# Reordered third-group products and DMA-turned q and k of unit 2 in a gated linear attention with a GEGLU block

## The chip, the cores and the metric

One core of a Trainium2 chip runs the whole program. The metric is the device time of one execution in microseconds (us). The engines are TensorE (PE; its weight loads are shown as PEld), VectorE (DVE), ScalarE (ACT), GpSimd (POOL) and SyncE (SP). SP and POOL also issue the DMAs; each issues in its own order.

## The reference

A recurrence over 768 steps for each of 4 batches and 8 heads of width 48, then a gated feed-forward block over the 3072 tokens that come out of it:

```python
mag = sqrt(a_re**2 + a_im**2)
a = (a_re + 1j * a_im) * min(mag, 0.999) / (mag + 1e-6)
for t in range(S):
    S_state = a[t][:, None] * S_state + outer(k[t], v[t])
    y[t] = q[t] @ real(S_state)
x = y as (B * S, 384)
g = x @ w_gate
gelu = 0.5 * g * (1 + erf(g / sqrt(2)))
ffn = (gelu * (x @ w_val)) @ w_out
out = x + sigmoid(x @ w_res) * ffn
```

The feed-forward width is 1536. All inputs are float32; the result is within the reference's type and shape, 3072 x 384 float32.

## The kernel before

**Groups and units.** The 768 steps of a batch are cut into three sections of 256 steps, two chunks of 128 each. A section of a batch is a *group*; there are 12, ordered by section and then by batch, so groups 0 to 3 are the first sections. Groups are gathered in *units*: unit 0 is group 0, unit 1 is groups 1 and 2, unit 2 is 3 and 4, unit 3 is 5 and 6, and so on, and unit 6 is group 11.

**The gates.** In a chunk the recurrence becomes a masked attention with q and k scaled by products of gates. The gates are handled as logarithm and angle. `squares` (lines L212 to L230) makes the sum of squares of a_re (tile `ar`) and a_im (tile `ai`): two squares, of which ScalarE does both for groups 0 and 5 and later, and one VectorE add into `lm`. `p1_steps` takes logarithms, a ratio and `p1_arctan` its arctangent. `cs_l` and `cs_t` sum logarithms and angles along the chunk by TensorE (L266, L299, L301); ScalarE turns the first sum into the tiles `E` and `Ei` and, by `p2_sin`, the second into sine and cosine, `CS`. The square of a_im of groups 5 and later is held in a buffer with the tag "E", of which there are two; `E` of each group and the square of earlier groups in the ramp use the same tag or others in turn.

**Products.** `products(g)` multiplies q by `E` (L360), k by `Ei` (L365), and each of these by `CS` into a padded tile of 128 columns per head, `padQ` and `padK` (L372). Two pads of each kind exist, used by even and odd groups.

**Attention.** It needs q and k with the step along the free axis. For groups below `TURN`, TensorE transposes them, four heads at a time (L450 for Q, L453 for K), into PSUM; ScalarE copies the Q half (L455) and VectorE the K half (L456) into SBUF, and then four score products follow (L460) and a mask (L463). From group `TURN` on, `products` issues on SP one transposing DMA for each pad (L376, tiles `QT` and `KT`), and the score products read those (L437, mask L440). Attention of groups below `TURN` is traced at high priority, that of later groups is not. The first unit has an attention of its own, `attention_first`, whose last masked score is remembered as `T["last"]`.

**Feed-forward.** For each unit and each of the 12 slices of the feed-forward width, `gv_step` makes a gate product `gp` (L586), a value product `vp` (L590), the gelu on ScalarE (L139, `h<-gp`) and a product on VectorE (L593), remembered as `T["gelu"]` and `T["gmul"]`. `rp_step` makes the residual gate (L602), and `op_step` the output product (L610), its scaling (L613), a store on SP (L617) and an accumulating store of x on POOL (L619).

**Stages and order.** After a ramp, the program runs for each unit u a phase X and a phase Y. Phase X of u holds the output products of unit u - 1, the second half of unit u's attention, the exponentials, angles and sines of unit u + 1, and the logarithms and arctangents of unit u + 2. Phase Y of u holds unit u's `gv_step`s, the products of unit u + 1 (`dec3` and `products`), the squares of unit u + 3 and the first half of unit u + 1's attention. `weave` merges the streams of a phase by hand: each stream has a begin and an end between 0 and 1, and its steps are spread between them. This written order gives priorities; the framework then puts the instructions of each engine into a fixed order at build time, in which an instruction may pass one of higher priority that isn't ready by the framework's own reckoning. On the chip each engine keeps that order. ScalarE's functions need table loads (L624), and `act` chains them so that they keep the written order.

**Fences in the order.** `issue_after(i)` puts the instructions that a block traces on i's engine behind i in that engine's queue; `paced(nm)` does so with the instruction remembered under a name, if there is one, and otherwise does nothing. It adds no wait between engines.

**Loads.** `load_a` (L159), `load_q` (L167) run on SP, `load_v` (L173) on POOL, the latter behind a one-element copy that waits for k's landing (L196, `landed`). The gate tiles have 4 (`ar`) and 6 (`ai`) buffers, q and k three each.

Of the kernel before, what the change touches and what calls it, by code (L numbers as in the profile page):

```python
# [16 lines left out]
def weave(*streams):  # L17

    order = []
    for si, (begin, end, steps) in enumerate(streams):  # L20
        n = len(steps)
        for i, step in enumerate(steps):
            order.append((begin + (end - begin) * (i + 0.5) / n, si, i, step))
    for _, _, _, step in sorted(order, key=lambda e: e[:3]):
        step()
# [3 lines left out]
def kernel(  # L29
# [23 lines left out]
    NG = B * NS  # L53
    UNITS = [[0]] + [[g, g + 1] for g in range(1, NG - 1, 2)] + [[NG - 1]]
    NU = len(UNITS)
# [2 lines left out]
    CHUNK = [b * NS + s for b, s in ORD]  # L58
    NEXT = {g: ORD.index((b, s + 1)) for g, (b, s) in enumerate(ORD) if s < NS - 1}
    P1AT = {2: -1}  # L60
    DVSQ = (1, 2, 3, 4)
    MAGIC = 12582912.0
    I2PI = 1.0 / (2.0 * math.pi)
    TURN = 5
    LATE0, LATE1 = 0.6, 1.0
    LNMAX = 0.5 * math.log(0.998001)

# [87 lines left out]
    def load_a(g, after=None):  # L155
        for nm, src, pool in (("ar", a_re, ldr), ("ai", a_im, lda)):
            t = pool.tile([128, C, H, D], FP, tag=nm, name=nm)
            for c in range(C):
                T["ld", nm, g] = held(nc.sync.dma_start(out=t[:, c], in_=rows(src, g, c)), after)  # L159
            T[nm, g] = t  # L160
        T["a"] = g + 1
# [71 lines left out]
    def p1_steps(g):  # L233

        def s0():
            lm = T["lm", g]
            act(out=lm, in_=lm, func=AF.Ln)
            nc.vector.tensor_scalar(out=lm, in0=lm, scalar1=0.5, scalar2=LNMAX, op0=OP.mult, op1=OP.min)  # L238

        def s1():  # L240
            ar = flat(T["ar", g])
            T["s", g] = pE.tile([128, W], FP, tag="E" if g == 1 else "Ei", name="ra") if g in (1, 2) else ar
            act(out=T["s", g], in_=ar, func=AF.Ln)

        def s2():
            T["th", g] = flat(T["ai", g])
            act(out=T["s", g], in_=T["s", g], func=AF.Exp, scale=-1.0)
            nc.vector.tensor_tensor(out=T["th", g], in0=T["s", g], in1=T["th", g], op=OP.mult)
        return [s0, s1, s2]

    def p1_arctan(g):
        act(out=T["th", g], in_=T["th", g], func=AF.Arctan)
# [374 lines left out]
    def gs(u):  # L627
        return UNITS[u] if 0 <= u < NU else []
# [7 lines left out]
    def call(f, *a):  # L636
        return lambda: f(*a)
# [4 lines left out]
    def att_steps(u, half):  # L642

        todo = [(g, c, i * C + c) for i, g in enumerate(gs(u)) for c in range(C)]
        n = len(todo) // 2
        steps = []
        for i, (g, c, jj) in enumerate(todo[half * n:half * n + n]):
            steps += attention(g, c)
            if i > 0:
                steps.insert(-1, call(xt_step, u, jj - 1))  # L650
        if n:
            steps.append(call(xt_step, u, half * n + n - 1))
        return steps

    def phase_x(u):

        pend = []
        g1 = gs(u + 1)
        p1g = [g for w in range(NU) if P1AT.get(w, w - 2) == u for g in gs(w)]
        now = [g for g in p1g if g in g1]  # L660
        ahead = [g for g in p1g if g not in g1]
        ops = [call(op_step, u - 1, jj) for jj in range(len(gs(u - 1)) * C)]
        att = att_steps(u, 1)
        if not g1:
            weave((0.0, 0.8, att), (0.1, 1.0, ops))
            return

        def csl(g, c):
            pend.append(cs_l(g, c))

        def ex():
            pend.pop(0)()

        def p1(g):
            return p1_steps(g) + [call(decay0, g)]
        csls = [call(csl, g, c) for g in g1 for c in range(C)]
        exs = [ex for _ in g1 for _ in range(C)]
        dec = [call(decay2, g) for g in g1]
        cst = [f for g in g1 for f in [call(carry, g)] + [call(cs_t, g, c) for c in range(C)]]
        sin = [call(p2_sin, g) for g in g1]  # L680
        table("natural_log_exp_and_others")()
        if now:
            atn = [table("trig_and_small")] + [call(p1_arctan, g) for g in now + ahead]
            pn = zip_steps([p1(g) for g in now])
            weave((0.0, 0.05, pn[:2]), (0.06, 0.1, csls), (0.12, 0.25, pn[2:]), (0.26, 0.4, exs),
                  (0.28, 0.48, zip_steps([p1(g) for g in ahead])),
                  (0.5, 0.5, dec), (0.55, 0.65, atn), (0.62, 0.8, cst), (0.9, 0.95, sin),
                  (0.0, 0.8, att), (0.0, 0.25, ops) if u == 1 else (0.1, 1.0, ops))
            return
        atn = [table("trig_and_small")] + [call(p1_arctan, g) for g in ahead]  # L690
        weave((0.0, 0.12, csls), (0.05, 0.5, zip_steps([p1(g) for g in ahead])), (0.12, 0.45, exs),
              (0.46, 0.46, dec), (0.2, 0.65, cst), (0.7, 0.95, atn + sin), (0.0, 0.8, att), (0.1, 1.0, ops))

    def ramp():

        g0, g1, g2 = gs(0) + gs(1)
        pend = {}

        def csl(g):
            pend[g] = [cs_l(g, c) for c in range(C)]  # L700

        def ex(g):
            for f in pend[g]:
                f()
            decay2(g)

        def cst(g):
            for c in range(C):
                cs_t(g, c)
        g3, g4 = gs(2)  # L710
        p = {g: p1_steps(g) for g in range(5)}
        q = {g: squares(g) for g in range(5)}
        pr = products(g0)

        def run(*fs):
            for f in fs:
                f()
        table("natural_log_exp_and_others")()
        run(*q[g0], p[g0][0], p[g0][1])
        csl(g0)  # L720
        run(p[g1][1], p[g0][2], q[g1][1], p[g1][2])
        ex(g0)
        run(p[g2][1], q[g2][1], p[g2][2])
        table("trig_and_small")()
        pr[0]()
        pr[2]()
        for g in (g0, g1, g2):
            if g > g0:
                T["f", g] = flat(T["ar", g])
            p1_arctan(g)  # L730
            cst(g)
            if g == g0:
                run(q[g1][0], q[g1][2], q[g2][0], q[g2][2])
        p2_sin(g0)
        pr[1]()
        pr[3]()
        a0 = attention_first(g0, 0, 0)
        table("natural_log_exp_and_others")()
        run(p[g1][0], p[g2][0])
        run(*a0[:2])  # L740
        csl(g1)
        csl(g2)
        run(*a0[2:4], *q[g3], p[g3][1], p[g3][2])
        ex(g1)
        run(*a0[4:7], *q[g4], p[g4][1])
        ex(g2)
        run(p[g4][2], p[g3][0], p[g4][0], call(decay0, g4), *a0[7:])
        with tc.issue_after(T["row"].ins):
            load_q(2, T["ld", "w", 2])
        load_w_out()  # L750
        table("trig_and_small")()
        p2_sin(g1)
        p2_sin(g2)
        with tc.issue_after(T["ld", "k", 2].ins):
            load_a(5)
        p1_arctan(g3)
        p1_arctan(g4)

    def phase_y(u):

        gv = []
        if 0 <= u < NU:
            table("gelu_and_others")()
            gv = [call(gv_step, u, f) for f in range(KF)]
            rp = [call(rp_step, u, jj) for jj in range(len(gs(u)) * C)]
            gv = gv[:8] + rp[:len(rp) // 2] + gv[8:] + rp[len(rp) // 2:]
        def late(f):
            with tc.issue_after(T["last"].ins):
                f()
        dec3 = [call(decay3, g) for g in gs(u + 1)]  # L770
        sq = [f for w in range(NU) if P1AT.get(w, w - 2) == u + 1 for g in gs(w) for f in squares(g)]
        pr = [st for g in gs(u + 1) for st in products(g)]
        if u == 0:
            pr = [call(late, f) for f in pr]
        weave((0.0, 1.0, gv), (0.0, 0.4, pr), (0.55, 0.56, dec3), (0.5, 0.95, sq), (0.3, 0.95, att_steps(u + 1, 0)) if u < 2 else (LATE0, LATE1, att_steps(u + 1, 0)))

    for g in range(3):
        load_a(g)
# [11 lines left out]
    for u in range(NU + 1):  # L790
        if u > 0:
            phase_x(u)
        while T["a"] < min(NG, gs(u + 1)[-1] + 6 if gs(u + 1) else NG):
            load_a(T["a"])
        phase_y(u)
        for g in gs(u + 2):
            with tc.issue_after(T["turn"].ins) if "turn" in T else nullcontext():
                load_q(g)
            after_landing(T["k", g], call(load_v, g))


# [28 lines left out]
```

## Time and profile before

Eight runs gave a median of 302.65 us (301.96 to 303.57). The profiled execution took 302.10 us by the same measure, of which 300.3 us are the span of the trace.

| engine | busy us | share of the span | instructions |
|---|---|---|---|
| PE | 256.7 | 85% | 1928 |
| DVE | 229.3 | 76% | 412 |
| ACT | 200.2 | 67% | 333 |
| POOL | 89.3 | 30% | 133 |

The mean granted clock of TensorE is 0.949 of full speed. The DMA queues moved 41.92 MB, 140 GB/s in the mean, nearly all in pieces under 512 B. The gelu tables are loaded at 57.11, 94.16, 138.36, 177.67, 218.68 and 252.96 us for units 0 to 5: these mark the stages. In the page's slices each digit is the busy share of a slice of 7.5 us in tenths; in a timeline the bracket behind a line gives the engine's idle time before it and what ended that. A busy PE is a PE with matmuls in flight, not one at its peak.

### The profile page before, as it was taken

What the parts mean: (1) busy time and instruction counts of PE and PEld (TensorE: products, weight loads), DVE (VectorE), ACT (ScalarE), POOL (GpSimd) and SP (SyncE); (2) the same over time, 40 slices, a digit from 0 to 9 for tenths busy, and PEclk for the clock granted to TensorE, in tenths of its full rate; (3) what the DMA queues carried; (4) which work ended last, traced back from release to release, by engine and by line L of the source; (5) the groups of instructions that cost most, each with busy time, mean ns of one, the idle gap of its engine ahead of it and who ended that gap; (6) DMA issues with size and microseconds to landing.
All of it is one profiled execution on the core that took longest, in us unless ns stands there. A gap on an engine that the chain in (4) does not pass through costs nothing.

```text
span 300.3 us, 5306 instructions
## 1 busy us (share of the span) xinstructions
PE 256.7 (85%) x1928; PEld 155.3 (52%) x1928; DVE 229.3 (76%) x412; ACT 200.2 (67%) x333; POOL 89.3 (30%) x133
## 2 busy tenths in 40 slices
PE   0345865599698999799999999989999998999994
PEld 0122543587354666454466654556545664455782
DVE  0789983989589999599897998888977776564452
ACT  3877788459989578996669964678464655445250
POOL 4020940400245520372113672125711222010220
PEclk9999575589979999999999999999999999999999
DMA  9999999999999993059999689998599735910631
GB/s 149 187 175 187 174 203 180 169 176 173 180 167 183 192 192 18 4 112 202 185 176 163 53 122 199 201 173 66 82 198 197 111 40 119 180 26 2 157 57 53
DMA packets 167427, 41.92 MB, mean 140 GB/s; under 512 B 156516, under 2 KB 167400, under 8 KB 167400
## 3 DMA queue, kind: packets, MB, share of 16 engines
q1 hardware_dynamic: 132424, 30.95, 62.1%
q0 software_dynamic: 34976, 10.63, 34.3%
q8 instruction: 15, 0.25, 0.3%
q14 instruction: 12, 0.10, 0.1%
HBM read 31.33 MB, written 9.08 MB: 135 GB/s over the span
## 4 chain that ended last, share of the span: by engine, by line
PE 67%; ACT 14%; DMA 8%; issue 4%; DVE 3%; SPq 2%; POOL 1%; ACTq 0%; DVEq 0%
PE op L610 15%; PE gp L586 15%; PE vp L590 14%; DMA q<-in_q_dram 4%; PE cst L299 4%; PE rp L602 3%; PE cst L301 3%; DMA wv<-in_moe_w_val_dram 3%; ACT L624 2%; PE at L437 2%; PE dk L479 2%; SPq L159 2%; ACT lm L139 2%; DMA ai<-in_a_im_dram 1%; ACT CS L139 1%
## 5 line engine op out<-in xcount | busy, mean ns | idle before, releaser
L139 ACT ACTIVATE h<-gp 128x512 bf16<-128x512 f32 (+1 forms) x84 | 44.7, 536 | 42.7 <-PE gp L586 42.2
L593 DVE SCALAR_TENSOR_TENSOR h<-h,vp 128x512 bf16<-128x512 bf16 (+1 forms) x84 | 50.4, 606 | 19.2 <-PE vp L590 15.2
L586 PE MATMUL gp<-xT,wg 128*128 128x512 bf16 (+1 forms) x252 | 62.8, 354 | 0.7 <-DVE xT L577 0.4
L590 PE MATMUL vp<-xT,wv 128*128 128x512 bf16 (+1 forms) x252 | 62.9, 354 | 0.0
L610 PE MATMUL op<-wo,h 128*128 128x384 bf16 x288 | 52.3, 333 | 2.5 <-ACT Ei L139 2.5
L619 POOL DMA_DIRECT2D out_dram<-x x22 | 19.8, 900 | 66.6 <-DMA out_dram<-ot 66.2
L610 PEld LDWEIGHTS <-h 128*128 128x128 bf16 x288 | 27.8, 99 | 21.3 <-issue 5.4
L590 PEld LDWEIGHTS <-wv 128*128 128x128 bf16 x252 | 24.5, 99 | 20.0
L586 PEld LDWEIGHTS <-wg 128*128 128x128 bf16 x252 | 23.8, 100 | 18.2 <-issue 1.2
L173 POOL DMA_DIRECT2D v<-in_v_dram x24 | 21.6, 906 | 29.1 <-DMA ai<-in_a_im_dram 23.8
L322 POOL DMA_DIRECT2D m<-d x32 | 23.4, 746 | 17.7 <-DMA d<-Ei 9.1
L624 ACT ACT_TABLE_LOAD x21 | 26.9, 1283 | 1.1 <-PEq L814 0.7
L266 PE MATMUL csl<-lm,lt0a 128*128 128x384 f32 x24 | 12.4, 602 | 11.1 <-DVE lm L238 11.1
L613 DVE SCALAR_TENSOR_TENSOR ot<-sg,op 128x384 f32<-128x384 f32 x24 | 13.2, 549 | 10.7 <-PE op L610 9.3
L440 DVE TENSOR_TENSOR atm<-at,mask 128x512 bf16<-128x512 f32 x28 | 19.1, 682 | 2.3 <-PE at L437 2.3
L196 POOL COPY landed<-k 1x1 f32<-1x1 f32 x9 | 2.1, 231 | 58.6 <-DMA k<-in_k_dram 58.6
L299 PE MATMUL cst<-ai,lt0b 128*128 128x384 f32 x24 | 11.7, 571 | 7.7 <-ACT ai L139 6.0
L360 DVE TENSOR_TENSOR q<-q,E 128x768 bf16<-128x768 f32 x12 | 11.4, 952 | 8.4 <-DMA q<-in_q_dram 4.6
L492 ACT CAST x<-y 128x384 bf16<-128x384 f32 x22 | 10.6, 480 | 11.0 <-PE y L489 10.8
L139 ACT ACTIVATE ar<-ar 128x768 f32<-128x768 f32 x20 | 16.7, 855 | 0.0
L230 DVE TENSOR_TENSOR lm<-lm,sq 128x768 f32<-128x768 f32 x12 | 11.4, 949 | 7.0 <-ACT sq L226 6.7
L139 ACT ACTIVATE CS<-ai,hpi 128x768 bf16<-128x768 f32 x12 | 11.2, 929 | 7.7 <-DVE ai L307 7.7
(112 smaller groups left out, 511.9 us busy)
## 6 DMA issues: line engine op xcount, KB each, us to landing
ar<-in_a_re_dram SPq DMA_DIRECT2D x24, 192.0 KB, 5.5
ai<-in_a_im_dram SPq DMA_DIRECT2D x24, 192.0 KB, 5.2
q<-in_q_dram SPq DMA_DIRECT2D x24, 192.0 KB, 4.7
k<-in_k_dram SPq DMA_DIRECT2D x24, 192.0 KB, 5.0
out_dram<-ot SPq DMA_DIRECT2D x24, 192.0 KB, 2.7
out_dram<-x POOLq DMA_DIRECT2D x22, 192.0 KB, 4.2
v<-in_v_dram POOLq DMA_DIRECT2D x24, 96.0 KB, 4.8
wg<-in_moe_w_gate_dram POOLq DMA_DIRECT2D x4, 288.0 KB, 6.7
```

The costliest lines, as they stand in the source:

```text
L139: return tab(nc.scalar.activation(**kw))
L173: held(nc.gpsimd.dma_start(out=t[:, c], in_=rows(v, g, c)), after)
L299: nc.tensor.matmul(out=cs, lhsT=tmat[c], rhs=th[:, sl], start=True, stop=(s == 0))
L322: nc.gpsimd.dma_start(out=m[u * D:(u + 1) * D].rearrange("p r h -> p (r h)"), in_=md.rearrange("r (h d) -> d (r h)", h=H))
L440: nc.vector.tensor_tensor(out=atm, in0=at, in1=mask4, op=OP.mult)
L586: nc.tensor.matmul(out=gp, lhsT=wg[:, fi, ffi * 128:(ffi + 1) * 128], rhs=xT[:, fi, :], start=(fi == 0), stop=(fi == KD - 1))
L590: nc.tensor.matmul(out=vp, lhsT=wv[:, fi, ffi * 128:(ffi + 1) * 128], rhs=xT[:, fi, :], start=(fi == 0), stop=(fi == KD - 1))
L593: T["gmul"] = nc.vector.scalar_tensor_tensor(out=h2[:, ffi, :], in0=h2[:, ffi, :], scalar=0.5, in1=vp, op0=OP.mult, op1=OP.mult)
L610: nc.tensor.matmul(out=ps, lhsT=h2[:, ffi, jj * 128:(jj + 1) * 128], rhs=wo[:, ffi, :], start=(ffi == 0), stop=(ffi == KF - 1))
L613: nc.vector.scalar_tensor_tensor(out=ot, in0=T["sg", u][:, jj], scalar=1.0, in1=ps, op0=OP.add, op1=OP.mult)
L619: nc.gpsimd.dma_start(out=out[t0:t0 + 128, :], in_=T["x", token(u, jj)], accum_op=OP.add)
L624: tab(nc.scalar.preload_act_table_set(nm))
```

## The change

Four things are changed.

- In phase Y of unit 0, the products of group 1 and of group 2 are two streams of `weave` now. Those of group 1 are spread from 0.0 to 0.15 and stay behind `T["last"]`; those of group 2 are spread from 0.35 to 0.6, each behind the `T["gmul"]` last traced.
- `TURN` is 3 and not 5: groups 3 and 4 get transposing DMAs, and their attention loses its high priority. In phase Y of unit 1 the first half of their attention is spread from 0.6 to 1.0, as in later units, and not from 0.3 to 0.95.
- `HELD` is group 6. Its squares leave phase Y of unit 0 and come at the head of its own steps in phase X of unit 1. Its gate load is traced at the end of the ramp, right behind group 5's.
- The loop at the end traces q, k and v loads of unit u + 2 first and gate loads behind them, both behind the last transposing DMA traced so far (`T["turn"]`); it keeps one group more ahead than before. In the pass of unit 0 no transposing DMA has been traced, so nothing is held there.

```diff
+    HELD = UNITS[3][-1]
...
-    TURN = 5
+    TURN = 3
...
         def p1(g):
-            return p1_steps(g) + [call(decay0, g)]
+            return (squares(g) if g == HELD else []) + p1_steps(g) + [call(decay0, g)]
...
         with tc.issue_after(T["ld", "k", 2].ins):
             load_a(5)
+            load_a(6)
...
-        def late(f):
-            with tc.issue_after(T["last"].ins):
+        def late(nm, f):
+            with paced(nm):
                 f()
         dec3 = [call(decay3, g) for g in gs(u + 1)]
-        sq = [f for w in range(NU) if P1AT.get(w, w - 2) == u + 1 for g in gs(w) for f in squares(g)]
-        pr = [st for g in gs(u + 1) for st in products(g)]
+        sq = [f for w in range(NU) if P1AT.get(w, w - 2) == u + 1 for g in gs(w) if g != HELD for f in squares(g)]
+        pr = [(0.0, 0.4, [st for g in gs(u + 1) for st in products(g)])]
         if u == 0:
-            pr = [call(late, f) for f in pr]
-        weave((0.0, 1.0, gv), (0.0, 0.4, pr), (0.55, 0.56, dec3), (0.5, 0.95, sq), (0.3, 0.95, att_steps(u + 1, 0)) if u < 2 else (LATE0, LATE1, att_steps(u + 1, 0)))
+            g1, g2 = gs(1)
+            pr = [(0.0, 0.15, [call(late, "last", f) for f in products(g1)]),
+                  (0.35, 0.6, [call(late, "gmul", f) for f in products(g2)])]
+        weave((0.0, 1.0, gv), *pr, (0.55, 0.56, dec3), (0.5, 0.95, sq), (0.3, 0.95, att_steps(u + 1, 0)) if u < 1 else (LATE0, LATE1, att_steps(u + 1, 0)))
...
-        while T["a"] < min(NG, gs(u + 1)[-1] + 6 if gs(u + 1) else NG):
-            load_a(T["a"])
         phase_y(u)
         for g in gs(u + 2):
-            with tc.issue_after(T["turn"].ins) if "turn" in T else nullcontext():
+            with paced("turn"):
                 load_q(g)
             after_landing(T["k", g], call(load_v, g))
+        while T["a"] < min(NG, gs(u + 1)[-1] + 7 if gs(u + 1) else NG):
+            with paced("turn"):
+                load_a(T["a"])
```

## The prediction

> **What bounds the kernel now.** I read the page's slices first, then the timeline of 43 to 62 us, then busy time by stage, then the groups of one stage, then SP's queue. The slices show where the clock and the DMA engines stand:
>
> ```profile
> PEclk9999575589979999999999999999999999999999
> DMA  9999999999999993059999689998599735910631
> ```
>
> A slice is 7.5 us. From slice 4 to 7 (30 to 60 us) TensorE is at half clock: it is not fed. The DMA engines are full to about 112 us and nearly empty from 112 to 127 us. So the front of the kernel lives on its loads, and there is a hole behind them. The hole in the compute is here:
>
> ```profile
> 50.01 1.56 ACT L139 ACTIVATE ai<-ai 128x768 f32<-128x768 f32 x2
> ...
> 52.51 0.96 DVE L360 TENSOR_TENSOR q<-q,E 128x768 bf16<-128x768 f32 x1 [4.57 <-DMA q<-in_q_dram]
> 53.38 0.95 DVE L372 TENSOR_TENSOR padQ<-CS,q 128x1536 bf16<-128x1536 bf16 x1
> ...
> 54.39 0.66 PE L450 MATMUL tp<-ident,padQ 128*96 128x128 bf16 x4 [3.68 <-DVE padQ L372]
> ...
> 56.51 0.58 ACT L455 COPY qk<-tp 96x512 bf16<-96x512 bf16 x1 [4.95 <-PE dk L479]
> 57.11 1.28 ACT L624 ACT_TABLE_LOAD   x1
> ```
>
> Columns are start, us, engine, line, operation; the bracket is the idle time before it and what ended it. VectorE has put the q product of group 2 ahead of group 1's Q product. It waits 4.57 us for group 2's q, issued at 44.03 and landed near 52.5. Group 1's inputs were ready when the sine of L139 ended, 47.72 + 0.83 = 48.55. TensorE and ScalarE wait in line behind it, and the gelu table of unit 0 is loaded only at 57.11. From there on the stages look like this (us, then busy time of PE, PEld, DVE, ACT, POOL, then clock, DMA share, GB/s):
>
> ```profile
> 94.20:120.30 26.10, 25.45 (x264) 15.97 (x263) 24.97 (x46) 19.48 (x35) 8.28 (x13) 1.00 1.07 136
> 120.30:137.70 17.40, 15.72 (x78) 8.97 (x77) 13.69 (x24) 15.45 (x25) 9.33 (x14) 1.00 0.45 71
> 137.70:158.90 21.20, 21.14 (x159) 11.30 (x158) 19.62 (x37) 14.64 (x26) 3.10 (x4) 1.00 1.21 193
> 158.90:178.40 19.50, 18.64 (x139) 11.65 (x139) 17.70 (x31) 17.57 (x28) 11.90 (x18) 1.00 0.96 107
> ```
>
> The first two rows are unit 1's products and the stage behind it, with unit 2's attention (groups 3, 4) turned by TensorE; the last two are the same work one unit on, turned by DMA. Both are held by PE and DVE, and the turned pair is shorter.
>
> **Group 2's products behind gelu products.** Nothing is added; four VectorE instructions of about 0.95 us move. Group 1's Q product can start at 48.55 instead of 53.38, 4.8 us earlier. With it go the first transposes (54.39 to 49.6), ScalarE's copy at 56.51 (to 51.7, just behind the arctans that end at 51.57) and the gelu table. Group 2's q and k have landed by about 54.1 (second k half issued at 48.6, shortest landing 5.5), before the fifth gelu product would come (near 59), so no wait takes this place. What is late next: group 2's attention starts after the fifth to eighth gelu product and not interleaved from the start. Its transposes began about 2 us apart (58.36, 62.04, 63.79, 65.60 ...); with padK at 63.5 its fourth set starts near 69.5 against 72.47 − 4.8 = 67.7, so 1.8 us of tail could remain. Its last x is read by TensorE only at 88.71, so I let the next stage hide most of it. Ends: 0 and −5.5; I take **−4.5**.
>
> **The clock** decides part of that. Row: PE restarts at 54.39 and the granted clock is 0.50 in 56 to 60, 0.78 in 60 to 64, so full from about 61.8, 7.4 us later. [...]
>
> **Unit 2 turned by DMA.** Removed, by the groups of 94.2 to 137.7 us:
>
> ```profile
> L453 PE MATMUL tp<-ident,padK 128*96 128x128 bf16 x32 | 3.4, 223 | 0.0
> ...
> L456 DVE COPY qk<-tp 96x512 bf16<-96x512 bf16 x8 | 3.3, 415 | 0.4 <-ACT qk L455 0.2
> ```
>
> In all 64 transposes, 16 copies. In the chain four transposes take 0.22 us, so 16 × 0.22 = 3.5 us of TensorE; VectorE loses 8 × 0.33 = 2.7 (spacing), ScalarE 8 × 0.5 = 4. TensorE is on the path: −3.5. From the neighbour: between gelu tables, 94.16 to 138.36 is 44.2 us, the next two intervals (138.36, 177.67, 218.68) are 39.3 and 41.0, mean 40.2: −4.0. The earlier y1 still waits for its own gelu table, so I take the smaller, **−3.5**; ends −5 and 0. The attention also loses its high priority, so group 4's half moves into the next stage, where PE has 1.7 us idle; the neighbour includes that.
>
> Added: four transposing DMAs on SP, each behind a pad product:
>
> ```profile
> 137.80 3.32 SPq L376 DMA_TRANSPOSE QT<-padQ  x1
> ...
> 147.97 4.09 SPq L376 DMA_TRANSPOSE KT<-padK  x1
> ```
>
> One is 128 × 2048 × 2 B = 0.52 MB. Here four take from 137.8 to their last landing at 154 to 156 (5.9 to 8.2 us after issue), some 4 to 4.5 us each. [...] The first pair lands about 10 us into the stage and is first read by PE at 149.25, 11.5 in: slack 1.5 us. The second lands 16 to 18 in and is read at 158.09, 20.4 in. [...] At unit 1 the DMA engines are full (1.40 share, 193 GB/s in 94.2 to 102); the deferral below is what clears them.
>
> **Loads.** Group 6's gate load keeps its place on SP (after group 2's k, behind group 5's). q and k of 3 and 4 pass ahead of group 7's gate load: about 3.4 us earlier (72.03 to 68.6), which covers most of the 4.8 us by which their use at 81.79 and later moves. Groups 7 and 8 land about where they do now, near 86 to 91, used after 100. q and k of 5, 6 and gates of 9, 10 wait on SP behind the last transpose, some 14 us into the stage (near 103): they fall into the hole of 112 to 127; products of 5 are needed near 125. POOL's v loads follow k's landing by a copy in its queue, as they already do one unit on (159.99). Cost 0; if the cover goes, each us of late q is a us.
>
> **Group 6's squares** leave unit 0's stage (two ScalarE squares of 0.73, one VectorE add of 0.87) for the next one, where ScalarE is busy 16.45 of 17.9 us and is the path: +1.5 at most, with an idle 1.19 us there (before L139 at 87.04) to take part: **+0.8**. Their data lands near 71.2, about when that stage now starts (76.3 − 4.5): no wait.
>
> Sum against the profiled 302.10: −4.5 − 3.5 + 0.8 = −7.2, 294.9. The median shown is 0.55 above that execution: **295.4**. Span 300.3 − 7.2 = 293.1.
>
> **Rivals.** (1) Group 2's chain ends last: the stall is only moved to the end of unit 0's stage. Then −3.5 + 0.8 and perhaps −1 remain: 299. For it: VectorE is 17.18 of 19.2 busy there. Against: 4.57 us of idle VectorE are really filled by group 1. 17%. (2) The transposes land late, behind gate loads of 7 and 8 still in flight, and PE waits in the turned attention: the second gain is gone, 302.65 − 4.5 + 0.8 = 299. Against: SP holds 0.4 MB less ahead of them than now. 13%. (3) Slower: the squares of group 6 need a buffer of tag E, of which there are two, and the same stage needs both for E of groups 3 and 4. Now they come a stage earlier, when both are free. If E of 4 is given its buffer first, the square waits for E of 3 to be released, that is for its row's transfer, issued by SP at 86.16 and landed 5.6 later. Group 6's logarithm stands in ScalarE's table order, so exponentials, sines and the gelu table all wait: the trig table, due 11.3 us into the stage, would come some 22 to 25 in, +11 to +13: 302.65 − 7.2 + 11 = 306. It decides from the moment E of 4 is given its buffer before the square. Against: the square precedes that exponential in the written order, and it frees the buffer after one add. 14%. Other disorder in the ordering, slower: 4%.
>
> **Chances.** Forecast 52% (291 to 297.5), (1) 17, (2) 13, (3) and disorder 18. Faster by over 0.3% (0.9 us, about what this measurement tells from no change) 0.78, within it 0.05, slower 0.17. The range, 290.5 to 301.5, leaves out most of (3) and a little beyond each end.
>
> **What would show it.** Right: padQ of group 1 starts near 48.6 with no DMA wait, gelu table near 52.5, gelu tables of units 1 and 2 near 89.5 and 130, no L450 or L453 after 80 us, L437 in their place without a DMA wait. Wrong: VectorE or ScalarE waiting at a square, a logarithm or the add of group 6; PE waiting for a transpose at L437; the gelu table of unit 1 still at 93 or later.

## The result and the profile after

The changed kernel takes 298.67 us (median of 11 runs, 297.11 to 300.67) against 302.64 for the kernel before in the same sessions. The ratio is 0.9864 with a 95% interval of 0.9844 to 0.9884: 4.0 us faster, where 7.2 were forecast. Its profiled execution took 300.16 us (span 298.4), so the trace explains 1.9 us of gain, and the execution in it is one of the slower ones; what made it slower is not settled (e10 below). Line numbers above L159 are one higher than before, and from L593 on another five higher in e6, e8, e9 and e10: L361, L366 and L373 are the products, L377 the transposing DMAs, L438 the turned scores, L227 the square of a_im, L587 and L591 gate and value products, L618 the store, L625 the table load. Ratios leave out runs that the comparison counted as disturbed, so with e2, e8 and e9, which had some, a ratio can stand a little off the quotient of the medians.

The slices of the page, to be held against those of before:

```profile
PEclk9999586995999799999999999999999999999999
DMA  9999999999995999959999879997799636910631
```

With slices counted from 0, the hole in the DMA row of before (3, 0 and 5 tenths in slices 15 to 17) is filled: 9, 9, 5. The queues move 44.00 MB instead of 41.92, which is four transposes of 0.52 MB more. The clock row is full earlier (9 in slices 7 and 8, from 52 us), but has a new 5 in slice 9 (67 to 75 us) and a 7 in slice 13 (97 to 104 us).

The timeline of the changed kernel (start, us, engine, line, operation; in the bracket the idle time before it and what ended that):

```profile
47.70 0.96 DVE L373 TENSOR_TENSOR padQ<-CS,q 128x1536 bf16<-128x1536 bf16 x1 [0.65 <-ACT CS L140]
...
51.17 1.28 ACT L625 ACT_TABLE_LOAD   x1
...
61.23 0.39 ACT L140 ACTIVATE h<-gp 128x256 bf16<-128x256 f32 x1
66.76 0.84 ACT L227 ACTIVATE sq<-ai 128x768 f32<-128x768 f32 x1 [5.14 <-DMA ai<-in_a_im_dram]
67.51 0.37 ACT L140 ACTIVATE h<-gp 128x256 bf16<-128x256 f32 x1
```

The first two lines are what was meant: group 1's Q product starts at 47.70 with no DMA in its bracket (before, its turn came at 53.38), and the gelu table of unit 0 is loaded at 51.17 instead of 57.11. The last three are the answer to that. In the kernel before, the same square had no wait:

```profile
69.53 0.85 ACT L226 ACTIVATE sq<-ai 128x768 f32<-128x768 f32 x1
```

In the changed kernel ScalarE, in its fixed order, reaches the square of group 5's a_im at 61.6, and stands there for 5.14 us until the load lands. The gelu behind it is late by as much, and so are VectorE's product with it and TensorE, which waits 5.38 us for that gelu until 67.93 and then runs at half clock to about 73 (the 5 in slice 9). The chain of waits (start, us, what) names the same thing:

```profile
54.78 11.90 DMA ai<-in_a_im_dram
...
66.76 0.84 ACT sq L227
```

Nothing delayed that load much: SP issued a_im of group 5 from 53.03 on before and from 53.48 on after, and by the completion signals of the DMA in the two traces its last part landed at 66.53 and at 66.68. Before, the square came at 69.53, 3.0 us behind the landing. What moved is the reader, by 7.9 us to 61.62. That is more than the 4.6 us of the stall, because ScalarE had six copies of transposes (L455) ahead of that square before and has four (L456) now; the others belong to group 2 and come later.

The table loads mark the stages. Times of the load in both profiled executions:

| table load | before | after | difference | length of the stage that ends there, before and after |
|---|---|---|---|---|
| gelu, unit 0 | 57.11 | 51.17 | −5.9 | |
| logarithm | 76.31 | 75.05 | −1.3 | unit 0's products: 19.2, 23.9 |
| gelu, unit 1 | 94.16 | 94.93 | +0.8 | stage behind: 17.9, 19.9 |
| logarithm | 120.26 | 116.64 | −3.6 | unit 1's products: 26.1, 21.7 |
| gelu, unit 2 | 138.36 | 135.41 | −3.0 | stage behind: 18.1, 18.8 |
| logarithm | 158.86 | 157.17 | −1.7 | unit 2's products: 20.5, 21.8 |
| gelu, unit 3 | 177.67 | 175.98 | −1.7 | stage behind: 18.8, 18.8 |

From there both run alike. About 0.9 of the 5.9 is an earlier start of the ramp's last part in this execution: the table load before this one stands at 44.33 instead of 45.21. So the first part gave what was asked of it and lost it in its own stage. The stage behind lost 2.0 more. The turned attention won 3.7 over two stages, and unit 2's products gave 1.3 of it back.

### The profile page after: what moved, and what is told of

Read it like the earlier page. It is cut to its first block, busy times and chain, and to the rows that moved or that the text cites. A ratio compares the mean times of both kernels' runs of the same rounds, so it can differ in the third digit from the quotient of the medians.

```text
span 298.4 us, 5172 instructions
## 1 busy us (share of the span) xinstructions
PE 251.3 (84%) x1864; PEld 151.0 (51%) x1864; DVE 226.6 (76%) x404; ACT 196.0 (66%) x325; POOL 89.7 (30%) x133
## 4 chain that ended last, share of the span: by engine, by line
PE 55%; ACT 15%; DMA 13%; DVE 7%; issue 4%; SPq 3%; POOL 1%; DVEq 0%; ACTq 0%; POOLq 0%
PE vp L591 14%; PE gp L587 14%; PE op L611 12%; DMA ai<-in_a_im_dram 5%; PE rp L603 3%; ACT L625 3%; DMA wv<-in_moe_w_val_dram 2%; SPq L160 2%; PE cst L300 2%; PE cst L302 2%; PE at L438 2%; DMA v<-in_v_dram 2%; DMA q<-in_q_dram 2%; ACT ar L140 2%; DMA ar<-in_a_re_dram 2%
## 5 line engine op out<-in xcount | busy, mean ns | idle before, releaser
L594 DVE SCALAR_TENSOR_TENSOR h<-h,vp 128x512 bf16<-128x512 bf16 (+1 forms) x84 | 50.6, 607 | 26.5 <-PE vp L591 18.1
L587 PE MATMUL gp<-xT,wg 128*128 128x512 bf16 (+1 forms) x252 | 63.2, 359 | 3.2 <-ACT h L140 1.8
L591 PE MATMUL vp<-xT,wv 128*128 128x512 bf16 (+1 forms) x252 | 63.2, 359 | 0.0
L611 PE MATMUL op<-wo,h 128*128 128x384 bf16 x288 | 50.7, 326 | 1.1 <-ACT Ei L140 0.7
L591 PEld LDWEIGHTS <-wv 128*128 128x128 bf16 x252 | 25.4, 101 | 23.2 <-issue 1.7
L620 POOL DMA_DIRECT2D out_dram<-x x22 | 19.9, 922 | 56.5 <-DMA out_dram<-ot 52.8
L611 PEld LDWEIGHTS <-h 128*128 128x128 bf16 x288 | 27.3, 98 | 17.9 <-issue 2.0
L587 PEld LDWEIGHTS <-wg 128*128 128x128 bf16 x252 | 24.3, 101 | 21.4 <-issue 4.7
L174 POOL DMA_DIRECT2D v<-in_v_dram x24 | 22.4, 939 | 30.0 <-DMA ai<-in_a_im_dram 23.9
L441 DVE TENSOR_TENSOR atm<-at,mask 128x512 bf16<-128x512 f32 x36 | 24.5, 682 | 2.3 <-PE at L438 2.3
L572 PE MATMUL tpx<-ident,x 128*128 128x128 bf16 x72 | 8.5, 234 | 10.1 <-ACT h L140 5.4
L603 PE MATMUL rp<-wr,xT 128*128 128x384 bf16 x72 | 15.7, 330 | 0.0
```

Of the source, the lines that this page charges most:

```text
L174: held(nc.gpsimd.dma_start(out=t[:, c], in_=rows(v, g, c)), after)
L441: nc.vector.tensor_tensor(out=atm, in0=at, in1=mask4, op=OP.mult)
L587: nc.tensor.matmul(out=gp, lhsT=wg[:, fi, ffi * 128:(ffi + 1) * 128], rhs=xT[:, fi, :], start=(fi == 0), stop=(fi == KD - 1))
L591: nc.tensor.matmul(out=vp, lhsT=wv[:, fi, ffi * 128:(ffi + 1) * 128], rhs=xT[:, fi, :], start=(fi == 0), stop=(fi == KD - 1))
L594: T["gmul"] = nc.vector.scalar_tensor_tensor(out=h2[:, ffi, :], in0=h2[:, ffi, :], scalar=0.5, in1=vp, op0=OP.mult, op1=OP.mult)
L603: nc.tensor.matmul(out=rp, lhsT=xT[:, fi, jj * 128:(jj + 1) * 128], rhs=wr[:, fi, :], start=(fi == 0), stop=(fi == KD - 1))
```

## Experiments

The theory (A) was that the gain of the split was given back at one wait, group 5's square for its load. The rivals were that the split was worth little anyway (B), and that transposes or squares cost what was won (C). All medians are against about 302.6 us for the kernel before.

**e1: the split undone, all else kept.**

```diff
-            pr = [(0.0, 0.15, [call(late, "last", f) for f in products(g1)]),
-                  (0.35, 0.6, [call(late, "gmul", f) for f in products(g2)])]
+            pr = [(0.0, 0.4, [call(late, "last", f) for g in (g1, g2) for f in products(g)])]
```

> The changed kernel, with the products of groups 1 and 2 in one stream again (0.0 to 0.4, all behind the first unit's last mask), so that VectorE should wait for group 2's q once more. Theory A (the gain in unit 0's stage was given back by the square of group 5's a_im, whose load lands near 66.7 us whatever comes before it): the wait for q comes back (about 4 us, gelu table near 57) and the wait at the square goes (below 1.5 us); the time rises by 0.5 to 1.5 us only, to about 299.7. Theory B (the split itself makes group 2's chain end last): the time falls to 297.5 or below. The prediction's own sum, with nothing given back: plus 4.5, about 303.

301.34 us, ratio 0.9955 [0.9938, 0.9971]. In its timeline VectorE waits for q of group 2 as before:

```profile
53.36 0.96 DVE L361 TENSOR_TENSOR q<-q,E 128x768 bf16<-128x768 f32 x1 [5.63 <-DMA q<-in_q_dram]
```

The gelu table is back at 57.97, and the square of a_im comes at 72.06 without a wait. In the changed kernel the split is worth 2.7 us, less than the forecast's 4.5 and more than the 0.5 to 1.5 that (A) allowed.

**e2: unit 2 turned by TensorE again, the split kept.**

```diff
-    TURN = 3
+    TURN = 5
...
-        weave((0.0, 1.0, gv), *pr, (0.55, 0.56, dec3), (0.5, 0.95, sq), (0.3, 0.95, att_steps(u + 1, 0)) if u < 1 else (LATE0, LATE1, att_steps(u + 1, 0)))
+        weave((0.0, 1.0, gv), *pr, (0.55, 0.56, dec3), (0.5, 0.95, sq), (0.3, 0.95, att_steps(u + 1, 0)) if u < 2 else (LATE0, LATE1, att_steps(u + 1, 0)))
```

> The changed kernel with groups 3 and 4 turned by TensorE as before (and their attention spread from 0.3 to 0.95 again, and so no transposing DMA to hold the loads of unit 1's pass). Theory A: the turn is where nearly all of the measured 4 us come from, so the time is 302 to 303 and the wait at group 5's square stays near 5 us. Theory B: same as A here. Rival C (the turn gave little, because the transposes and the half clock at the start of unit 1's stage ate it): 299 to 300.

Median 302.6 us with a wide spread (299.29 to 305.08 in 12 runs), ratio 0.9975 [0.9950, 1.0001]. Its profiled run waits 3.46 us at the square of group 5's a_im, not the 5 of the expectation. With the transposes goes the hold of the loads in the pass of unit 1, so what is priced is both together. By the ratios the turn is worth 0.0111 × 302.6 = 3.4 us in the changed kernel, by the medians 3.9. That agrees with the forecast's 3.5, within the about 1 us that this spread leaves open.

**e3: both groups of unit 3 held, so that group 5's squares also leave unit 0's stage.**

```diff
-    HELD = UNITS[3][-1]
+    HELD = UNITS[3]
...
-            return (squares(g) if g == HELD else []) + p1_steps(g) + [call(decay0, g)]
+            return (squares(g) if g in HELD else []) + p1_steps(g) + [call(decay0, g)]
```

> The changed kernel with group 5's squares held back to the next stage too, like group 6's. Theory A: ScalarE's 5.1 us at the square of a_im in unit 0's stage are gone, its logarithm table comes near 70 instead of 75.05, and the next stage is longer by 1 to 2 us (two more squares, and loads that arrive as it needs them); the time is 295 to 297. Theory B: the stage of unit 0 still ends near 74 because group 2's attention ends it; 298 to 299.5.

295.49 us, ratio 0.9751 [0.9725, 0.9776]: 3.2 us below the changed kernel. No wait stands at a square, and unit 0's stage is 18.1 us instead of 23.9.

**e4: the square stays, its load gets the queues.** While group 5's a_im is under way, POOL issues the three loads of the output weights (2.36 MB read), from 53.49 on. This kernel issues them only when that a_im has landed; the first output product that reads them starts at 82.28.

```diff
-                 T["ld", "q", 2])
+                 T["ld", "ai", 5])
...
-        load_w_out()
         table("trig_and_small")()
...
             load_a(6)
+        load_w_out()
         p1_arctan(g3)
```

> The changed kernel with the loads of w_out (three transfers on POOL, 2.36 MB read) held until group 5's a_im has landed, instead of until group 2's q has. Theory A: a_im of group 5 then lands near 58 to 60 instead of 66.7, no wait at its square is left, and the time is 294.5 to 296.5, unless w_out becomes late for the first output product (needed near 80, should land near 75). Theory B: no change, 298 to 299.5.

295.12 us, ratio 0.9749 [0.9718, 0.9780]. From its timeline:

```profile
60.04 2.27 POOL L190 DMA_DIRECT2D wo<-in_moe_w_out_dram  x3 [5.86 <-DMA ai<-in_a_im_dram]
...
64.89 0.87 ACT L227 ACTIVATE sq<-ai 128x768 f32<-128x768 f32 x1
```

The a_im has landed near 60 instead of near 66.7, with the same issue time (53.55), and the square at 64.89 has no bracket. The stage is 18.8 us. Two different edits, one moving the reader and one hastening the load, take away the same wait and give the same 3.2 to 3.5 us. So the core of (A) holds: the wait at that square is what the split gave back. Against e1, in which nothing waits there either, the split is now worth 5.9 to 6.2 us; that is an estimate, because e1 was not run with the edit of e3 or e4.

**e5: e4 with group 6's squares back in unit 0's stage** (`HELD = None` instead of `HELD = UNITS[3][-1]`), to price their move.

> The kernel of e4_wo_late with no group held: group 6's squares are back in unit 0's stage. Theory A, extended (the 2 us by which the stage from 75.05 to 94.93 grew over that of before are the held squares: VectorE and ScalarE chains of group 6 come late in it): that stage, 20.2 us between tables in e4_wo_late, is 18 to 18.5 long, unit 0's stage is 0.5 to 1.5 us longer, and the time is 0.5 to 1.5 us below e4_wo_late's 295.1. Rival (the stage grew because loads of q, k, a_re arrive when it needs them): the stage stays near 20 us and the time is 295 to 296.

298.19 us, ratio 0.9849 [0.9826, 0.9872], 3.1 us slower than e4. The stage behind does shrink, to 18.4 us from 20.2 in e4. But now group 6's load is the late one:

```profile
71.04 0.84 ACT L227 ACTIVATE sq<-ai 128x768 f32<-128x768 f32 x1 [5.28 <-DMA ai<-in_a_im_dram]
```

In these two profiled runs the hold costs 1.8 us in one stage and saves a wait of 5.28 in the stage ahead of it. In e4 and e5 the output weights are issued when group 6's a_im is under way (from 61.16 on in e5; its second half lands at 70.93), so part of that wait may be e4's own doing; e8 below has the same order up to there and waits 0.81.

**e6: e4 with TensorE kept busy at the start of unit 1's products.** Busy time by stretch (length; then busy us and count for PE, PEld, DVE, ACT, POOL; then granted clock, DMA share, GB/s) shows, in the changed kernel, where the 7 in the clock row is from:

```profile
94.00:96.00 2.00, 0.75 (x9) 0.45 (x9) 2.00 (x4) 1.98 (x3) 0.00 (x0) 1.00 0.51 133
96.00:98.00 2.00, 1.13 (x4) 0.50 (x4) 2.00 (x4) 1.30 (x4) 1.88 (x3) 0.82 1.16 209
98.00:100.00 2.00, 2.00 (x6) 0.72 (x5) 0.80 (x3) 0.59 (x1) 0.38 (x1) 0.50 0.67 69
100.00:102.00 2.00, 2.00 (x9) 0.78 (x8) 1.49 (x3) 0.60 (x2) 0.00 (x0) 0.83 1.40 250
```

TensorE is idle for 1.05 us at 94.2 and for 1.07 at 95.8, where its own transposes used to stand. Then the clock is halved, and a gate or value product of three matmuls follows the next after some 1.28 us instead of 0.65. The edit puts eight matmuls behind the second value product of unit 1, into a PSUM tile that nothing reads:

```diff
+        if u == 1 and ffi == 1:
+            idle = psT.tile([128, 512], FP, tag="tp", name="idle")
+            with tc.issue_after(mv.ins):
+                for _ in range(8):
+                    nc.tensor.matmul(out=idle, lhsT=ident, rhs=xT[:, 0, :], start=True, stop=True)
```

> The kernel of e4_wo_late with eight matmuls (128x512, result unused) put on TensorE behind the fourth product of unit 1, where it waits for the gelu table. It is for the half clock: in e4_wo_late the clock is 0.50 from 94 to 96 us and 0.8 beside it, and four products of three take 1.3 to 1.5 us and not 0.65. If those idle 2.1 us bring the half clock, it stays at 1.0 and unit 1's stage is 1.5 to 2 us shorter (19.8 to 20.2 between tables, not 21.7), the time 293 to 294. If TensorE's clock there has nothing to do with the idle time, or VectorE holds that stage anyway, 295 to 296.

294.73 us, ratio 0.9734 [0.9710, 0.9758]. The clock is 1.00 from 57.4 us on, and unit 1's products, which start at 89.70 here, take 20.0 us instead of 21.7. But of these 1.7 us only 0.4 reach the end, less than the two intervals tell apart. Unit 2's products are 23.6 us long where e4 has 22.4. A line from VectorE's timeline there:

```profile
128.95 0.56 DVE L619 SCALAR_TENSOR_TENSOR ot<-sg,op 128x384 f32<-128x384 f32 x1 [2.45 <-DMA out_dram<-ot]
```

The output tile waits for an earlier store to leave, the next scaling is late as well, and TensorE waits 0.65 us for it (until 132.58); e4 has no such wait. SP issued that unit's first stores at 126.07, behind the gate loads of groups 9 and 10, which sit since the change at the very end of the held loads and were issued up to 126. Compute that comes earlier runs into SP's queue in this run, and in those of e8 and e9 (0.42 and 1.80 us at the same scaling); e10 does not show it.

**e7: the hold behind the transposes taken away for the one pass where it matters most.**

```diff
-            with paced("turn"):
+            with paced("turn") if u != 1 else nullcontext():
                 load_q(g)
...
-            with paced("turn"):
+            with paced("turn") if u != 1 else nullcontext():
                 load_a(T["a"])
```

> The changed kernel, but the loads traced in the pass of unit 1 (q and k of groups 5 and 6, gates of 9 and 10) are not put behind the last transposing DMA. The prediction's rival 2 (loads in flight make the transposes late): the transposes of groups 3 and 4 start 2 to 6 us later on SP and TensorE waits for them at the score products; 299.5 to 302. If the hold isn't needed: 298 to 299.3.

306.83 us, ratio 1.0133 [1.0108, 1.0158]: slower than the kernel before. The same two events in the changed kernel and in e7:

```profile
94.41 2.09 SPq L377 DMA_TRANSPOSE QT<-padQ  x1
...
107.30 0.39 PE L438 MATMUL at<-QT,KT 96*128 96x128 bf16 x4
```

```profile
100.81 4.65 SPq L377 DMA_TRANSPOSE QT<-padQ  x1
...
111.45 0.61 PE L438 MATMUL at<-QT,KT 96*128 96x128 bf16 x4 [4.98 <-DMA KT<-padK]
```

With gate loads and loads of q and k ahead of it on SP, the first transpose starts 6.4 us later, TensorE stands 4.98 us for the K half, and unit 1's products take 28.6 us instead of 21.7. The hold is worth 8.2 us. It is what makes the turn pay at all: without it the turned kernel is 4.2 us slower than e2, which has no turn (302.6).

**e8 and e9: can the parts be added up?** e8 is e6 with `HELD = None`. e9 is e8 with the output weights held behind a_im of group 6 instead of group 5.

> The edits of e5_unheld and e6_warm together on e4_wo_late. If both theories hold and add up: 291.5 to 293. If only the matmuls help: 293 to 294; if neither, 295 to 296.

> The kernel of e8_unheld_warm with the loads of w_out held until group 6's a_im has landed, not group 5's. If e5's loss was only the wait for group 6's a_im (5.3 us at its square), that wait is below 0.5 us in every run, unit 0's stage is about 18.5 us, the next one 17.7 to 18.5, and the time is 292 to 294.3 with a narrower spread than e8's 293.2 to 298.4. If w_out then comes too late for the first output product (needed near 78): 294.5 to 297.

e8: 294.76 us, ratio 0.9725 [0.9687, 0.9763], the same as e6. Its stage behind unit 0 is 17.7 us, 2.2 shorter than in e6, and unit 1's products are 21.5, 1.5 longer: they start earlier, and TensorE waits 1.26 us until 100.97 for a K half that is still under way. Its square of group 6 waits 0.81 us where e5's waited 5.28, with the same instructions in the same order up to there. So with the matmuls the hold is worth nothing that these runs tell apart, without them 3.1 us; why is not settled. e9: 296.49 us, ratio 0.9760 [0.9718, 0.9803], six runs from 292.82 to 298.50. The expectation was missed. Its profiled run was the fastest, waited at neither square and had full clock from 84 to 106. The median lies where the expectation put output weights that come too late; in the profiled run their last part landed at 76.57, just as the first output product ran (76.16), without a wait. What the other runs waited for isn't seen, and stays open.

**e10: the changed kernel with e6's eight matmuls only.**

> The changed kernel with the eight matmuls of e6_warm and nothing else. If the half clock at the start of unit 1's stage is a cost of the change by itself: that stage is about 20 us between tables and not 21.7, and the time 296.8 to 297.8 (1 to 2 us below 298.67); if what the clock gives is taken back behind it by stores and loads in SP's queue, as e6_warm's small gain suggests: 298 to 298.7.

298.15 us, ratio 0.9851 [0.9818, 0.9884]: 0.5 us below the changed kernel, which the intervals don't tell from nothing, nor surely from the 1.7 us. Its profile shows two things. Unit 1's products take 20.0 us at full clock, as in e6; unit 2's products are as long as in the changed kernel (21.8), so in this profiled run nothing of the 1.7 is taken back. And the wait at the square is less than half as long in this execution, though each engine has the same instructions in the same order as in the changed kernel, but for the eight matmuls, which come after it:

```profile
66.27 0.84 ACT L227 ACTIVATE sq<-ai 128x768 f32<-128x768 f32 x1 [2.25 <-DMA ai<-in_a_im_dram]
```

The load landed at 66.19 here and at 66.68 in the changed kernel's run, nearly alike. What differs is when ScalarE arrives: at 64.02 against 61.62, behind a start 0.9 us later and TensorE at half clock from 54.3 to 57.7. So a shorter wait is not a shorter stage by as much: the logarithm table comes 1.3 us earlier, not 2.9. In both runs the rest of the stage starts with the landing. The changed kernel's spread of 3.6 us and a median 1.5 below its profiled run are not explained by this.

The fastest versions are e3, e4, e6 and e8 at 294.7 to 295.5 us. Their intervals overlap; all beat both kernels.

## Why the prediction was right, and where its sum was off

The direction and the two causes of the gain were right. The size was 7.2 us forecast and 4.0 measured; 298.67 lies inside the range but outside the band of 291 to 297.5 that was held most likely, and next to the 299 of rivals 1 and 2, neither of which took place. The signs were mixed as well. Group 1's padQ and the first gelu table came as said, and the scores of unit 2 read the turned tiles without a DMA wait. But the gelu tables of units 1 and 2 came at 94.93 and 135.41, not near 89.5 and 130; "still at 93 or later" had been named as a sign of being wrong. The largest part of the difference lies in one step, the first below.

- **The split.** The step that failed is "so no wait takes this place". It compared landing times with the new times of group 2's q and k, and later of group 6's squares. Group 5's squares were not looked at, though they stand in the stage that was moved by 5 us: the time of before, 69.53, less some 5, is about 64 to 65. That load landed at 66.53 in the trace of before, so its slack was 3.0 us, less than the shift. No wait shows this, as nothing waited for it there; its completion signals do, and its issue from 53.03 on, with full DMA engines (a mean share of 1.10 in 52.6 to 67.6) and the output weights issued beside it from 53.02 to 56.6, was a reason to look. Forecast −4.5; measured −2.7 as it is (e1) and, as an estimate, −5.9 to −6.2 with the wait gone (e1 against e3 and e4). The starts themselves came as said: padQ at 47.70 against 48.6, the table at 51.17 against 52.5, no wait at group 2's products (58.14 to 62.34).
- **"Cost 0" for the loads** holds for what it was said of, the held ones. The output weights, which keep their issue time on POOL, were not counted as traffic beside a load that had just lost its slack. e4 shows what that was worth.
- **The turn.** Forecast −3.5; measured −3.4 to −3.9 (e2), and −3.7 in the two stages (44.2 to 40.5 us). TensorE's own transposes no longer fill the gap at the start of unit 1's stage; that halved the clock (0.50 in 98 to 100 us; 1.00 with the eight matmuls of e6 and e10) and took 1.7 us (21.7 against 20.0). I had not foreseen that. Without it the two stages take 39.0 us in e6 (e10: 38.8), so the exchange itself was worth more than the neighbouring stages suggested. Unit 2's products then took 1.3 us longer than before, whose cause was not separated.
- **Group 6's squares.** Forecast +0.8; the stage grew by 2.0, and by 0.6 in e5, where they are elsewhere. The square stands at 79.87 and its add's logarithm at 84.21, in the middle of ScalarE's order. Whether the move is right is not settled: taken back it costs 3.1 us in e5 against e4, where their load is late in the old place, and nothing in e8 against e6.
- **Rival 1**, group 2's chain as the new end of the stage, is out: with the wait gone the stage is shorter than before (18.1 and 18.8 against 19.2). **Rival 2**, the transposes behind loads, is what e7 makes, with other loads (q and k of groups 5 and 6, gates of 9 and 10); in the changed kernel the hold prevents it. **Rival 3**, a blocked buffer, doesn't appear: the trigonometric table comes 13.9 us into the stage, not 22 to 25.
- **The clock at the restart.** I took the row of before, where 7.4 us lie between the restart (54.39) and the full clock (61.8): 57.0 for a restart at 49.6, an estimate. In the changed kernel it was full already near 49.5 (0.63 granted in 48 to 50), 3.3 us after the matmul at 46.15, so that estimate was 7.5 us too late. But e4 stood at 0.50 from 48 to 56 and at 0.61 in 56 to 60, and e10, whose code there is that of the changed kernel, fell back to 0.58 in 54 to 56. The time for this stretch is uncertain by about a microsecond at least: e4 and e6 differ by 0.9 us in unit 0's stage (18.8 and 17.9), with full clock for good from about 59 and 57. The low end of the range also allowed 2 us for a clock that is full sooner; no run shows that amount, and these 0.9 us are what the runs show in its place.

That the total of the forecast, 295.4, is what e3 and e4 reach is partly luck: a larger split makes up for larger squares and the half clock.

## What to carry to other kernels

When a stall is taken out of a stage, what stands behind it comes earlier, by the stall or, where the order changed too, by more (here 7.9 us for a stall of 4.6). So every load that the stage reads, and not only those of the moved step, has to be set against its new time. A load that nothing waited for has its landing in the trace all the same, in its completion signals (here 66.53 us in the trace of before). Where a load is late by little, look at what else the DMA engines carry meanwhile and whether that can wait: here a weight load that nothing read before 82 us cost 3.5. In these runs transposes by DMA paid only because the loads that would have stood ahead of them in the same queue were held back (306.83 us without the hold in e7, 298.67 with it, about 302.6 without the turn in e2), and in e6 the held loads in turn became what the stores stand behind (2.45 us of wait at one scaling).

## What the runs showed of the hardware

- **The clock fell on two short gaps.** In the traces of the kernel before and of the changed kernel the record of the granted clock has stretches at one level whose lengths are whole multiples of 3.41 us (before 6.83, 20.48 and 3.41, after 6.83, 17.07 and 3.41 among them), but for the last, which the end cuts off. With the busy time cut along these steps, the changed kernel's fall at the start of unit 1's stage looks like this:

```profile
93.85:97.27 3.42, 1.30 (x12) 0.65 (x11) 3.42 (x5) 3.39 (x5) 1.15 (x2) 1.00 0.78 169
97.27:100.68 3.41, 3.41 (x9) 1.22 (x8) 2.21 (x4) 0.76 (x3) 1.11 (x2) 0.50 0.85 127
100.68:104.09 3.41, 3.41 (x17) 1.57 (x16) 2.61 (x6) 1.67 (x3) 0.00 (x0) 1.00 1.48 186
```

No gap was longer than 1.07 us here: a piece in which TensorE was busy for 1.30 of 3.42 us was followed by one at half clock. With eight matmuls more in this place the clock stayed at 1.00 (e6, e10). How little work is too little is not shown: pieces with 1.80, 1.88 and 2.11 us of work were followed by half clock (before from 37.83, e10 from 50.90, e6 from 50.55), one with 1.60 by full clock (before from 24.18).
- **The same code, another clock.** The changed kernel's profiled run and e10's, the same up to about 92 us, had granted clocks of 1.00 and 0.57 at 56 to 58. The same load landed at 66.68 and 66.19; the waits for it, 5.14 and 2.25 us, differ by the reader.
- **One load's latency under traffic.** The second half of group 5's a_im took 11.9 us from issue to landing (the chain's piece at 54.78) with the output weights under way. In e4, without them, both halves, issued in 53.55 to 55.48, had landed by 60.0. The median of such loads on the changed kernel's page is 4.6. By the completion signals, that half took 9.2 to 12.6 us in all seven profiled runs with the output weights beside it (12.4 in the kernel before), and 4.6 to 5.3 in the five with the weights held back (e4, e5, e6, e8, e9).
